# A depthwise convolution and a SiLU expert on one core: the order of a block's products, of the first blocks and of SyncE's transfers

## The chip, the cores and the metric

The kernel runs on one core of one Trainium2 chip, in float32. The metric is the device time of one execution in microseconds; lower is better. The core's engines each run their own instruction stream: TensorE (PE, with its weight loads PEld), VectorE (DVE), ScalarE (ACT), GpSimd (POOL) and SyncE (SP), which issues most DMAs here.

## The reference

A causal convolution of seven taps along the sequence, with softmaxed taps for each of eight heads, and behind it a two-layer expert with a SiLU.

```python
x: (8, 4096, 192)   weight: (8, 7)   w_in: (192, 2048)   w_out: (2048, 192)
w   = softmax(weight, axis=-1)
y[b, s, h, :] = sum_k w[h, k] * x_pad[b, s + k, h, :]     # 6 zeros ahead
h   = y.reshape(32768, 192) @ w_in
out = (h / (1 + exp(-h))) @ w_out                          # (32768, 192)
```

## The kernel before

The 32768 rows are cut into 32 blocks of 1024 (two halves of 512, which lie on the two halves of the partitions). For each block the kernel turns x into a channel-major tile `xt` (L425), adds the taps on it (L456 to L461), copies the result into `dup` (L478), forms differences of it in `win` (L495 to L511), multiplies by combined input weights, sums the results up, puts them through SiLU into `g`, and multiplies those by combined output weights. Both matrix products are done with fewer products than the plain method, in the manner of Strassen: 15 products P0 to P14 instead of 18 for each of five groups of weights, and six output products D0 to D5, for each of four quarters j and two halves e of the hidden values.

Block 0 is done plainly (`up_plain`, `down_plain`) while weights are still being rounded and combined (`rounded` on VectorE, `combine` and `combine_out` on GpSimd). From block 1 on, the order on every engine is written out by hand: `PLAN` is a list of tokens, `step(b, token)` emits one token's instructions, and `pin` keeps the instructions of an engine in the order of emission. Instructions without `pin` may be moved by the framework. A token's prefix shifts its block: none is the block b of the loop, `-` is b - 1, `=` is b - 2 and `+` is b + 1. The bars in the list have no effect on the order.

| token | what it emits | engine, line |
|---|---|---|
| `Pr.g` | product r of group g, 64 rows deep, on one half of the array | PE L583 |
| `L.nk` | the plain part of the input product | PE L595 |
| `Di.je` | output product i of quarter j, half e: four matmuls on four parts of the columns; D5 has a quarter of the width | PE L687 |
| `u`, `S`, `SL` | copy of a chain's partial sum out of its bank; SiLU | ACT L619, L631, L636 |
| `X`, `a`, `b` | sums of partial results | DVE L615 |
| `t.ji` | differences of g for the output products | DVE L123 |
| `M`, `z`, `y`, `x`, `o`, `st` | merge of the output sums, transpose back, store | DVE L758, ACT L738 to L746, DVE L768, SP L776 |
| `ld.k`, `i.k`, `ha`, `v.ki`, `sp.k`, `w.i` | for the block after: load, transpose, halo (copy and two DMAs), tap i of part k, spread into dup, window steps | SP L140, DVE L425, SP L447 and L435, DVE L458/L461 or ACT L456, SP L478, DVE L495 to L511 |

(`ld` loads the block after as well.) The products of a group run in three chains, each in one PSUM bank: 5, 2, 6, 1, 0, 14; then 3, 9, 7, 4, 8; then 12, 10. In the first chain, ScalarE copies the sum out after nearly every member (`u5` after P5, `u2` after P6 and so on), and the next product may only write when that copy is done. P13 and P11 add into a bank that an X sum has filled. P pairs run side by side when one lies on each half of the array; `ON_B` says which products lie on the second half.

Of the kernel before, what the change touches and what calls it, by code (L numbers as in the profile page):

```python
# [9 lines left out]
F32 = mybir.dt.float32  # L10
# [7 lines left out]
def kernel(  # L18
# [63 lines left out]
        "P5.0 | -P8.3 ld.1 -t.20 | -D2.10 -t.21 | -D4.11 ld.2 | -D3.10 -w.0 -a0.3 | -D5.11 | "  # L82
        "-D4.10 -S0.3 | -D0.31 -t.23 | -D3.11 -t.22 | -D2.20 i.1 | -D5.10 | -D5.20 | -D0.30 "
        "-t.30 | -D1.11 i.2 | -D4.20 -w.1 | -D4.21 -w.2 -t.31 | -D3.21 | -D2.21 i.0 | -D5.21 "
        "ha.0 -t.33 | -D3.20 | -D2.31 -t.32 | -D1.00 -w.3 | -D2.30 -w.4 | -D0.00 v.10 | "
        "-D0.10 v.00 v.01 | -D3.31 -z1.0 v.02 -y0.0 | -D5.30 | -D1.20 u5.0 -M1.0 v.11 | "
        "-D4.31 -M2.0 | -D5.31 | -D3.30 -x2.3 -x2.2 -y1.0 | P2.0 | L.02 -M3.0 -y2.0 -w.5 | "
        "-D4.30 u4.0 -M6.0 -x0.0 | P6.0 | P3.0 -M4.0 v.12 | L.00 | P5.4 u2.0 X2.0 | L.01 | "
        "P1.0 u5.4 v.03 | P9.0 | P2.4 SL.0 -M5.0 -x2.0 -x2.1 | L.10 v.04 u0.0 | L.11 -o.1 "
        "-x1.0 | L.12 u4.4 | P0.0 | P13.0 X4.0 SL.2 -M7.0 | P12.0 | P6.4 u1.0 v.20 | P3.4 | "  # L90
        "P14.0 b1.0 u2.4 S2.0 v.21 | P1.4 | P7.0 S3.0 X2.4 | P11.0 | P10.0 a5.0 | P5.1 | "
        "P9.4 S4.0 b5.0 u0.4 | P4.0 | P13.4 X4.4 u5.1 v.13 | P12.4 | P0.4 a1.0 | P2.1 | P7.4 "
        "u1.4 -o.2 | P11.4 | P8.0 b1.4 u4.1 -st.2 a5.4 S5.0 | P14.4 | P6.1 S2.4 a0.0 | P10.4 "
# [38 lines left out]
    def load(b, ks=range(NK)):  # L132
        if b not in nats:
            nats[b] = nats[b % 2] if b > 1 else xpool.tile([P, NK, TB // SQ, SQ], F32, tag="nat", name="nat", bufs=2)
        nat = nats[b]
        for k in ks:
            for i in range(P // SQ):
                c = R * k + SQ * (i % 2)
                queue = nc.scalar if not b and k == 0 and i % 2 == 0 else nc.sync
                ins = queue.dma_start(  # L140
                    out=nat[SQ * i : SQ * i + SQ, k, :, :],
                    in_=x_v[2 * b + i // 2][:, :, c : c + SQ],
                )
                if not b:
                    pin(ins)
# [286 lines left out]
    def tail_of(b):  # L432
        if (b + 1) * TT % S:
            tails[b + 1] = xpool.tile([R, NK, pad], F32, tag="tail", name="tail", bufs=2)
            nc.sync.dma_start(out=tails[b + 1], in_=xts[b][R:P, :, TB : TB + pad])  # L435

    def halo_in(b, _):
# [9 lines left out]
        nc.sync.dma_start(out=xt[R:P, :, 0:pad], in_=xt[0:R, :, TB : TB + pad])  # L447
        tail_of(b)

    def conv(b, k, i):  # L450
# [4 lines left out]
        if i == 0 and b < 2:  # L455
            pin(nc.scalar.activation(dst, src, AF.Copy, scale=tap))  # L456
        elif i == 0:
            pin(nc.vector.tensor_scalar(dst, src, scalar1=tap, scalar2=None, op0=ALU.mult))  # L458
# [9 lines left out]
    def spread(b, k):  # L468
# [77 lines left out]
    bk, us, sums, cmbs, accs = {}, {}, {}, {}, {}  # L546
# [61 lines left out]

    def sums_h(b, name, g):
# [29 lines left out]
    def sum_g(b, j, i):  # L639
# [14 lines left out]
        engine = pool if f"t.{j}{i}" in ON_POOL else vec  # L654
        engine.tensor_tensor(t[i // 2][:, i % 2, :], u, v, op=ALU.subtract)
# [117 lines left out]
    def store_out(b, i):  # L773
        for q in range((HD if b else P) // SQ):
            n, c = (i % 2, HD * (i // 2) + SQ * q) if b else (q // 2, R * i + SQ * (q % 2))
            nc.sync.dma_start(  # L776
# [270 lines left out]
```

## Time and profile before

| what | us |
|---|---|
| median of 3 runs (2412.71 to 2414.83) | 2413.17 |
| the profiled execution, its own time | 2414.33 |
| its span | 2412.6 |
| TensorE busy | 2389.5 |
| VectorE busy | 2140.6 |
| ScalarE busy | 1148.0 |
| median from issue to landing, copies into dup | 2.3 |
| the same, stores of the output | 2.0 |

The lines of the profile stand for one execution. A group's count in L583, L595 and L687 is twice the number of matmuls, since each float32 product is recorded as two passes. "Idle before" is the time that an engine had nothing to do ahead of an instruction, with what released it. Line L123 is the helper behind pinned instructions, so those are told apart by tile.

### The profile page before, as it was taken

Reading aid. Unit: us, or ns where it says so; the run is one execution under the profiler, and the core shown is the slowest. Engines: PE = TensorE matmul, PEld = TensorE weight load, DVE = VectorE, ACT = ScalarE, POOL = GpSimd, SP = SyncE. Lnnn points to the kernel's source line nnn. Section 1 sums busy time; section 2 is a strip of 40 time slices with the busy share of each in tenths; the row PEclk is TensorE's granted clock in tenths of the full one; section 3 lists DMA queues with packets and bytes.
Section 4 is the critical chain, followed back from the end, with each engine's and each line's share of the span. In section 5 each row is a group of like instructions: output and inputs, shape, how many; then the busy total and the mean of one; then the engine's idle time right before and its main releaser. Section 6 shows DMA issues by size and latency. Waiting matters only on the chain.

```text
span 2412.6 us, 43590 instructions
## 1 busy us (share of the span) xinstructions
PE 2389.5 (99%) x17630; PEld 981.1 (41%) x17630; DVE 2140.6 (89%) x2967; ACT 1148.0 (48%) x2184; POOL 116.7 (5%) x168
## 2 busy tenths in 40 slices
PE   9799999999999999999999999999999999999998
PEld 5244433444433444334444334443344443344433
DVE  8789888999888998889998889988899988899876
ACT  5145444455444554444554445544445544455443
POOL 5900000000000000000000000000000000000000
PEclk9999999999999999999999999999999999999999
DMA  7411222221222212222212222122222122221111
GB/s 150 80 38 31 37 46 41 52 46 26 45 42 48 52 31 36 46 42 51 48 24 44 42 48 51 29 39 46 42 51 49 24 44 42 48 51 29 26 33 18
DMA packets 451242, 106.54 MB, mean 44 GB/s; under 512 B 423584, under 2 KB 428704, under 8 KB 451040
## 3 DMA queue, kind: packets, MB, share of 16 engines
q1 hardware_dynamic: 447392, 101.78, 23.1%
q8 instruction: 138, 2.26, 0.4%
q0 software_dynamic: 448, 1.58, 0.3%
q10 hardware_dynamic: 3200, 0.39, 0.1%
q14 instruction: 64, 0.52, 0.1%
HBM read 31.46 MB, written 25.17 MB: 23 GB/s over the span
## 4 chain that ended last, share of the span: by engine, by line
PE 94%; DVE 4%; SPq 1%; DMA 1%; issue 0%; ACT 0%; DVEq 0%; ACTq 0%
PE ps L687 47%; PE ps L583 45%; PE ps L595 2%; DVE two L123 1%; DVE nat L461 1%; DVE mh L123 1%; DMA dup<-nat 0%; SPq L776 0%; SPq L140 0%; DMA xt<-xt 0%; DVE win L495 0%; DMA nat<-in_x_dram 0%; DVE xt L425 0%; DVE wo L123 0%; DVE t L123 0%
## 5 line engine op out<-in xcount | busy, mean ns | idle before, releaser
L583 PE MATMUL ps<-win,ws 64*128 64x512 f32 x1550 | 703.2, 610 | 13.6 <-DVE ps L615 12.9
L687 PE MATMUL ps<-g,wo 128*32 128x512 f32 x2976 | 708.7, 594 | 0.0
L583 PE MATMUL ps<-win,wr 64*128 64x512 f32 x1550 | 656.5, 609 | 0.7 <-ACT u L619 0.7
L619 ACT COPY u<-ps 128x512 f32<-128x512 f32 x775 | 450.4, 586 | 207.6 <-PE ps L583 191.4
L687 PE MATMUL ps<-t,wo 128*32 128x512 f32 (+2 forms) x4528 | 543.6, 446 | 0.0
L687 PE MATMUL ps<-t,wx 128*32 128x512 f32 x2976 | 491.7, 594 | 0.1
L631 ACT ACTIVATE g<-g 128x512 f32<-128x512 f32 x465 | 279.2, 628 | 438.8 <-DVE g L615 438.8
L461 DVE SCALAR_TENSOR_TENSOR nat<-xt,taps,nat 128x512 f32<-128x512 f32 x564 | 422.4, 754 | 7.8 <-ACT nat L456 3.8
L583 PE MATMUL ps<-dup,wr 64*128 64x512 f32 x868 | 411.4, 593 | 0.8 <-POOL wr L319 0.8
L123 DVE TENSOR_TENSOR t<-g 128x1024 f32<-128x1024 f32 x248 | 301.7, 1217 | 54.5 <-PE ps L687 53.7
L583 PE MATMUL ps<-dup,ws 64*128 64x512 f32 x682 | 345.7, 603 | 0.0
L123 DVE TENSOR_TENSOR t<-g,t 128x1024 f32<-128x1024 f32 x248 | 302.3, 1220 | 46.0 <-PE ps L687 44.9
L583 PEld LDWEIGHTS ps<-win,wr 64*128 64x128 f32 x1550 | 234.5, 186 | 234.5 <-issue 86.7
L615 DVE TENSOR_TENSOR g<-u,ps 128x512 f32<-128x512 f32 x465 | 313.7, 680 | 15.0 <-PE ps L583 14.1
L583 PEld LDWEIGHTS ps<-win,ws 64*128 64x128 f32 x1550 | 240.5, 186 | 173.4 <-DVE ps L615 64.1
L631 ACT ACTIVATE g<-ps 128x512 f32<-128x512 f32 x465 | 263.6, 596 | 56.4 <-PE ps L583 56.4
L687 PEld LDWEIGHTS ps<-t,wo 128*32 128x32 f32 x4528 | 179.2, 110 | 239.3 <-issue 228.6
L615 DVE TENSOR_TENSOR ps<-u,ps 128x512 f32<-128x512 f32 x310 | 214.0, 690 | 58.0 <-ACT u L619 26.2
L687 PE MATMUL ps<-g,wx 128*32 128x512 f32 x1488 | 246.8, 595 | 0.0
L687 PEld LDWEIGHTS ps<-t,wx 128*32 128x32 f32 x2976 | 115.5, 110 | 269.4 <-issue 261.1
L687 PEld LDWEIGHTS ps<-g,wo 128*32 128x32 f32 x2976 | 162.0, 110 | 135.4 <-issue 135.4
L746 ACT COPY cmb<-ps 96x512 f32<-96x512 f32 x30 | 17.4, 581 | 418.9 <-PE ps L687 418.9
(90 smaller groups left out, 1831.4 us busy)
## 6 DMA issues: line engine op xcount, KB each, us to landing
dup<-nat SPq DMA_DIRECT2D x345, 128.0 KB, 2.3
nat<-in_x_dram SPq DMA_DIRECT2D x382, 64.0 KB, 2.5
out_dram<-osb SPq DMA_DIRECT2D x376, 64.0 KB, 2.0
raw<-in_moe_w_out_dram SPq DMA_DIRECT2D x8, 384.0 KB, 4.0
raw<-in_moe_w_in_dram SPq DMA_DIRECT2D x12, 192.0 KB, 4.6
ws<-wr POOLq DMA_DIRECT2D x8, 192.0 KB, 4.0
raw<-in_moe_w_in_dram SPq DMA_DIRECT2D x6, 128.0 KB, 3.1
xt<-xt SPq DMA_DIRECT2D x31, 4.5 KB, 1.9
```

The costliest lines, as they stand in the source:

```text
L123: return lambda *args, **kw: pin(getattr(self.engine, name)(*args, **kw))
L461: nc.vector.scalar_tensor_tensor(out=dst, in0=src, scalar=tap, in1=dst, op0=ALU.mult, op1=ALU.add)
L583: nc.tensor.matmul(to, raw(g, *LEFT[e][r], e), rhs, start=first, stop=True, skip_group_check=True)
L595: nc.tensor.matmul(banks[PLAIN_BANKS[n and 1 + e]][:, cols], rows(wr[j] if own == e else ws[j], e)[:, a, k, :], rows(dups[b], e)[:, SLOT[e ...
L615: pin(nc.vector.tensor_tensor(out_, u, v, op=op))
L619: pin(nc.scalar.copy(us[b, g, o], t1))
L631: pin(nc.scalar.activation(h, src, AF.Silu))
L687: nc.tensor.matmul(accs[b][at][SQ * q : SQ * q + SQ, to], lhs[:, e, SQ * k : SQ * k + SQ], rhs[:, e, ts(q, TB // 4) if i == 5 else to], st ...
L746: pin(nc.scalar.copy(c[0], acc[0][0:n, :]))
```

## The change

The loop's list `PLAN` is replaced by another order of the same 300 tokens. A second list, `START`, is walked once with b = 2 and gives the order from the end of block 0 through block 2; the loop then begins at b = 3. The list `FIRST` and the mixing of block 0's output product with block 1's taps go. The first tap of every part is computed on ScalarE for all blocks, where it was on VectorE from block 2 on. All DMAs of SyncE (loads, tails, halos, spreads, stores) and the t differences are pinned, and the head of the halo is copied by pinned ScalarE instructions in blocks 1 and 2. The ten u buffers are allocated once and taken in turn from a list. Counted in D tokens, the runs of D in a block were 29, 1, 2, 2 and 14 and become 12 and 36; in `START` they are 2, 5, 11, 18, 11 and 1.

```diff
@@ -79,38 +79,72 @@
     PLAN = (
-        "P5.0 | -P8.3 ld.1 -t.20 | -D2.10 -t.21 | -D4.11 ld.2 | -D3.10 -w.0 -a0.3 | -D5.11 | "
-        "-D4.10 -S0.3 | -D0.31 -t.23 | -D3.11 -t.22 | -D2.20 i.1 | -D5.10 | -D5.20 | -D0.30 "
-        "-t.30 | -D1.11 i.2 | -D4.20 -w.1 | -D4.21 -w.2 -t.31 | -D3.21 | -D2.21 i.0 | -D5.21 "
-        "ha.0 -t.33 | -D3.20 | -D2.31 -t.32 | -D1.00 -w.3 | -D2.30 -w.4 | -D0.00 v.10 | "
...
-        "X2.2 SL.1 S1.4 v.14 | P1.2 | P9.2 S4.1 a1.1 | P5.3 | P13.2 b5.1 u0.2 X4.2 | P8.1 | "
-        "P0.2 u5.3 v.22 S0.0 | P2.3 | P12.2 u1.2 v.23 | D0.01 a0.1 u4.3 S2.2 v.06 | D0.11 "
-        "S1.0 b1.2 S5.4 | P3.3 | P6.3 t.00 S0.1 | P11.2 | P7.2 u2.3 X2.3 | P10.2 | P1.3 S4.2 "
-        "a5.2 | P9.3 | P14.2 u0.3 b5.2 | P13.3 | P4.2 X4.3 S3.2 S1.1 v.24 | P0.3 | P12.3 "
-        "S5.1 v.15 | P11.3 | P7.3 u1.3 a1.2 | D1.01 b1.3 S1.2 a5.3 S4.3 | D0.21 S2.3 t.02 | "
-        "P8.2 | P14.3 v.25 | P4.3 | P10.3 sp.0 t.01 | D1.31 a0.2 | D1.21 t.03 S0.2 | D1.10 "
-        "S3.3 S5.2 t.10 | D2.01 | D2.00 v.16 | D4.01 a1.3 sp.1 b5.3 | D3.00 v.26 S5.3 | "
-        "D0.20 S1.3 t.11 sp.2 | D4.00 | D3.01 t.12 | D1.30 +ld.0 t.13 | D5.00 | D2.11 | "
-        "D5.01"
+        "P5.0 v.20 -t.01 | -P10.3 -S3.2 | -P4.3 -S1.1 -S0.1 -sp.2 -a0.2 | -D1.31 u5.0 -t.03 "
+        "-S4.3 | -D2.01 -S2.3 -t.02 | -D2.00 | -D0.00 -b5.3 | -D4.00 -a1.3 -S5.3 -t.10 -S5.4 "
+        "| -D3.01 -S0.2 -S5.2 | -D5.00 -w.0 | -D1.00 v.00 -t.11 -S1.2 | -D0.31 | -D1.30 -w.1 "
+        "| -D4.01 | -D2.10 -t.13 | -P8.3 | P2.0 v.11 | -D5.01 u4.0 v.01 | -D3.00 -S1.3 -t.12 "
+        "| -D4.10 | -D4.11 -t.20 | -D2.11 | -D3.10 -t.22 | -D5.11 | -D0.10 -a0.3 | -D0.11 "
...
+        "-D5.31 -M3.0 | -D5.21 | -D5.30 | -D4.30 -w.5 -M6.0 | -D5.20 | -D4.31 -x2.2 -x0.0 "
+        "-M4.0 | P3.0 | P6.0 -x2.0 -x2.1 v.15 | L.01 | P5.4 u2.0 -M5.0 | L.00 | P1.0 X2.0 "
+        "u5.4 v.26 | L.02 | P2.4 u0.0 v.04 | P0.0 | P9.0 SL.0 -w.4 -x1.0 | L.10 u1.0 X4.0 | "
+        "L.12 u4.4 -o.1 | L.11 -x2.3 | P14.0 | P13.0 v.16 -st.1 SL.2 -o.3 | P11.0 | P7.0 "
+        "S3.0 | P6.4 | P12.0 +ld.2 S4.0 a5.0 S2.0 | P5.1 | P3.4 b1.0 u2.4 | P4.0 | P10.0 "
...
+        "b5.1 u0.2 | P11.1 | P9.2 u2.3 a0.1 | P0.2 | P12.2 +i.1 S4.1 +ha.0 X4.2 | P1.3 | "
+        "P3.3 u1.2 b1.2 | P11.2 | P7.2 u0.3 -st.3 X2.3 S1.4 | P10.2 | P0.3 a5.2 S4.2 | P9.3 "
+        "-st.0 | P14.2 b5.2 u1.3 S5.1 -o.2 | P13.3 | P4.2 X4.3 -st.2 | P12.3 | P14.3 a1.2 | "
+        "P7.3 | P11.3 b1.3 S3.3 sp.0 +v.10 | P8.2 a5.3"
     )
-    ON_POOL = "".split()
+    START = (
+        "=i.2 =i.0 =i.1 =ha.0 -ld.2 =v.00 =v.10 =v.01 -ld.1 =v.20 =v.11 =v.21 =v.12 -ld.0 "
+        "=v.22 =v.23 =v.13 =v.14 =v.15 =v.02 =v.16 =v.24 =sp.1 =v.03 =v.25 =v.26 =v.04 =sp.2 "
+        "=v.05 =v.06 -i.2 =sp.0 -i.0 ld.1 =w.0 =w.1 =o.0 -i.1 -L.01 -P5.0 =w.2 -ha.0 -L.02 "
+        "-P5.4 -u5.0 =w.3 -P3.0 -P2.0 -u5.4 =w.5 =o.1 -L.00 -P2.4 -u4.0 =w.4 =st.1 -P6.0 "
+        "-u4.4 -SL.0 -P6.4 -u2.0 -X2.0 -L.11 -u2.4 -L.10 -v.10 -P12.0 -P1.0 -v.11 -L.12 -u0.0 "
+        "=o.2 -P9.0 -P1.4 -v.20 =st.2 -SL.2 -P13.0 -P0.0 -u0.4 -X4.0 -v.12 -P0.4 -P3.4 -u1.0 "
+        "ld.0 -S2.0 -b1.0 -P7.0 -P14.0 -u1.4 -X2.4 -P11.0 -P10.0 -S3.0 -a5.0 =st.0 -P5.1 "
+        "-P9.4 -S4.0 -b5.0 -v.13 -P12.4 -P4.0 -u5.1 ld.2 -X4.4 -v.00 -P2.1 -P14.4 -b1.4 -a1.0 "
...
+        "-S5.0 -P7.2 -P11.2 -v.24 -S0.1 -P9.3 -P14.2 -b1.2 -S5.4 -a5.2 -S1.4 -P10.2 -P1.3 "
+        "-S3.2 -v.25 -S5.1 -D0.00 -v.15 -S4.2 -v.05 -u0.3 -D1.00 -b5.2 -P0.3 -P13.3 -X4.3 "
+        "-v.16 -P12.3 -P4.2 -u1.3 -t.00 -P11.3 -P7.3 -a1.2 -D1.20 -b1.3 -S1.2 -D0.11 -a5.3 "
+        "-S2.3 -S4.3 -t.02 -D0.01 -S5.2 -D1.01 -v.26 -t.01 -D0.31 -v.06 -P10.3 -P14.3 -t.03 "
+        "-P8.2 -P4.3 -S3.3 -sp.2 -D1.21 -a0.2 -a1.3 -D1.30 -b5.3 -sp.1 -D0.21 -t.10 -S5.3 "
+        "-S0.2 -D4.00 i.1 -D3.01 i.0 +ld.2 i.2 -D4.01 -t.11 -D2.00 ha.0 -D2.01 -D0.20 -sp.0 "
+        "-t.12 -D3.00 -t.13 v.00 -D5.00 v.20 P5.0 -P8.3 -D5.01 -a0.3 -D2.10 -t.20 -S0.3 +ld.0 "
+        "-D5.11 -D4.10 -S1.3 v.21 v.10 -D1.10 u5.0 -w.0 -D2.11 -t.21 -D0.10 -w.1 -D3.10 v.01 "
...
+        "P1.3 S2.2 b1.2 P7.2 P11.2 -st.1 u0.3 X2.3 S1.4 P10.2 P14.2 +i.2 S4.2 a5.2 P0.3 P9.3 "
+        "+i.1 P13.3 P4.2 u1.3 X4.3 +ha.0 S5.1 b5.2 P14.3 P7.3 a1.2 P11.3 P12.3 S3.3 sp.0 a5.3 "
+        "S0.4 P8.2 b1.3 +v.10 -st.3"
+    )
     QUEUE = (0, 4, 1, 2, 3)
-    FIRST = (
-        ". | . | . | v.10 | . | v.11 | . | v.12 | . | v.13 | . | v.14 | . | v.15 | . | v.16 | "
-        ". | v.20 sp.1 | . | v.21 | . | v.22 | . | v.23 | . | v.24 | . | v.25 | . | v.26 | . "
-        "| sp.2 | . | . | . | . | . | . | . | . | w.0 | w.1 | w.2 | w.3 | w.4 | w.5 | . | ."
-    )
...
                 c = R * k + SQ * (i % 2)
                 queue = nc.scalar if not b and k == 0 and i % 2 == 0 else nc.sync
-                ins = queue.dma_start(
-                    out=nat[SQ * i : SQ * i + SQ, k, :, :],
-                    in_=x_v[2 * b + i // 2][:, :, c : c + SQ],
-                )
-                if not b:
-                    pin(ins)
+                pin(
+                    queue.dma_start(
+                        out=nat[SQ * i : SQ * i + SQ, k, :, :],
+                        in_=x_v[2 * b + i // 2][:, :, c : c + SQ],
+                    )
+                )
...
-            nc.sync.dma_start(out=tails[b + 1], in_=xts[b][R:P, :, TB : TB + pad])
+            pin(nc.sync.dma_start(out=tails[b + 1], in_=xts[b][R:P, :, TB : TB + pad]))
...
-            if b == 2:
+            if b <= 2:
                 pin(nc.scalar.copy(head, tails.pop(b)))
             else:
                 nc.gpsimd.tensor_copy(head, tails.pop(b))
-        nc.sync.dma_start(out=xt[R:P, :, 0:pad], in_=xt[0:R, :, TB : TB + pad])
+        pin(nc.sync.dma_start(out=xt[R:P, :, 0:pad], in_=xt[0:R, :, TB : TB + pad]))
         tail_of(b)
...
-        if i == 0 and b < 2:
+        if i == 0:
             pin(nc.scalar.activation(dst, src, AF.Copy, scale=tap))
-        elif i == 0:
-            pin(nc.vector.tensor_scalar(dst, src, scalar1=tap, scalar2=None, op0=ALU.mult))
...
-                    nc.sync.dma_start(out=rows(dups[b], e)[:, slot, :], in_=rows(src, n))
+                    pin(nc.sync.dma_start(out=rows(dups[b], e)[:, slot, :], in_=rows(src, n)))
...
+    us, free = {}, []
+
+    def used(*key):
+        free.append(us.pop(key))
+        return free[-1]
+
...
-            us[b, g, o] = upool.tile([P, TB], F32, tag="u", name="u")
+            us[b, g, o] = free.pop(0)
             pin(nc.scalar.copy(us[b, g, o], t1))
         elif name[0] == "X":
-            add(banks[XBANK[o]], us.pop((b, g, o)), t2)
+            add(banks[XBANK[o]], used(b, g, o), t2)
         elif name[0] == "a":
...
-        engine = pool if f"t.{j}{i}" in ON_POOL else vec
-        engine.tensor_tensor(t[i // 2][:, i % 2, :], u, v, op=ALU.subtract)
+        pin(nc.vector.tensor_tensor(t[i // 2][:, i % 2, :], u, v, op=ALU.subtract))
...
-            nc.sync.dma_start(
-                out=out_v[2 * b + n][:, :, c : c + SQ], in_=osbs[b][SQ * q : SQ * q + SQ, i, :, :]
+            pin(
+                nc.sync.dma_start(
...
-        if (b, token) == (1, "ha.0"):
-            assert not any(t[0] == "D" for c, t in did if c == 1)
-            for j in range(NJ):
-                combine_out(j)
...
-        y, x_ = (upool.tile([P, TB], F32, tag="u", name="u") for _ in range(2))
+        y, x_ = free[0:2]
...
-    ahead = [f"i.{k}" for k in range(NK)] + ["ha.0"] + [f"v.0{i}" for i in range(K)]
-    for t in ahead:
-        step(0, t)
     for g in (0, 1, 4, 2, 3):
         for e in range(2):
             combine(g, e)
-    step(0, "sp.0")
-    load(2)
-    beside = FIRST.split("|")
-    for _, s in zip_longest(down_plain(0), beside, fillvalue=""):
-        for t in s.split():
-            step(0, t)
-    for k in range(NK):
-        turn_out(0, k)
-        store_out(0, k)
-    did.update((0, t) for t in base if t[0] not in "ivw")
-    did.update((1, t) for t in base if t[:2] == "ld")
-
-    banks = [bank() for _ in range(8)]
+    ahead = {"i", "ha", "v", "sp", "w"}
+    outs = {f"{t}.{k}" for t in ("o", "st") for k in range(NK)}
+    did.update((0, t) for t in base if t.split(".")[0] not in ahead and t not in outs)
+
+    def first_down():
+        for _ in down_plain(0):
+            pass
+        for j in range(NJ):
+            combine_out(j)
+        banks.extend(bank() for _ in range(8))
+        free.extend(upool.tile([P, TB], F32, tag="u", name="u") for _ in range(10))
+
     begun = set()
-    for b in range(1, NB + 2):
+    for t in START.split():
+        if not banks and (t[:2] in ("-P", "-L", "=o")):
+            first_down()
+        step(2, t)
+    for b in range(3, NB + 2):
         for s in plan:
             for t in s:
                 step(b, t)
```

## The prediction

> **What bounds the kernel now.** I read the page first (busy shares and the forty slices), then the chain of waits, whole and for one block, then the timeline of each engine around the one hole that the slices show, and last the table by stage for the clock in that hole.
>
> ```profile
> PE 2389.5 (99%) x17630; PEld 981.1 (41%) x17630; DVE 2140.6 (89%) x2967; ACT 1148.0 (48%) x2184; POOL 116.7 (5%) x168
> PE   9799999999999999999999999999999999999998
> ```
>
> TensorE is busy 99% of the span; one slice, the second, is at 7. VectorE is close behind at 89%, ScalarE has half of its time free. So a gain must come from TensorE: from the hole, or from time in which it is "busy" but not at its rate. The chain of waits for the block at 930 to 1012 us shows the latter (start, length, line; L583 is the products P, L687 the output products D, a "x" counts half products, since each product is recorded as two passes):
>
> ```profile
> 959.34 1.85 PE ps L687 x16
> 961.20 6.33 PE ps L583 x28
> 967.52 1.85 PE ps L687 x16
> 969.38 1.92 PE ps L583 x8
> 971.29 10.88 PE ps L687 x112
> 982.17 1.06 PE ps L583 x4
> 983.23 21.19 PE ps L687 x232
> ...
> 1005.48 0.99 PE ps L687 x8
> ```
>
> Inside one kind, passes start every 0.429 us (timeline: 971.68, 972.11, then 972.96, 973.39), two P side by side, four parts of a D side by side. So a pair of P, or one D, takes 0.858 us, and a D5 a quarter of it. By that, x16 of D (two tokens) should take 1.72 and takes 1.85; x8 of P (two pairs) should take 1.72 and takes 1.92; x4 should take 0.86 and takes 1.06. A D run thus costs 0.13 to 0.14 extra and a P run 0.20: **0.34 us for each change to D and back**. The old list has five D runs in a block (of 29, 1, 2, 2 and 14 tokens), hence 1.7 us. The whole of it: 75 P at 0.429, six L at 0.429, 40 D at 0.858 and 8 D5 at 0.215 make 70.8 us; the period is 73.71 (first long P run of the second block at 127.03, of the last at 2338.23, thirty periods). Of the 2.9 us over, 1.7 are changes of kind and 1.2 are short waits of P for ScalarE's and VectorE's copies and sums.
>
> The hole:
>
> ```profile
> 108.44 1.02 PE L583 MATMUL ps<-win,ws 64*128 64x512 f32 x2
> 122.39 1.22 PE L583 MATMUL ps<-win,ws 64*128 64x512 f32 x1 [12.93 <-DVE ps L615]
> ...
> 106.69 6.34 SPq L776 DMA_DIRECT2D out_dram<-osb  x12
> 113.14 0.63 SPq L447 DMA_DIRECT2D xt<-xt  x1
> ...
> 115.14 1.25 DVE L458 TENSOR_SCALAR nat<-xt,taps 128x512 f32<-128x512 f32 x2 [5.51 <-DMA xt<-xt]
> 116.42 5.32 DVE L461 SCALAR_TENSOR_TENSOR nat<-xt,taps,nat 128x512 f32<-128x512 f32 x4
> 121.65 0.68 DVE L615 TENSOR_TENSOR ps<-u,ps 128x512 f32<-128x512 f32 x1
> ```
>
> Read it backwards. TensorE waits 12.93 us for an X sum (L615); that sum stands on VectorE behind six taps of block 2; those wait 5.51 us for the halo copy (L447); and the halo copy stands on SyncE behind twelve stores of block 0. The hole costs more than itself:
>
> ```profile
> 113.80:122.30 8.50, 0.00 (x0) 0.00 (x0) 7.06 (x8) 0.00 (x0) 7.88 (x14) 0.50 0.20 29
> 122.40:127.30 4.90, 4.90 (x18) 3.22 (x20) 3.13 (x4) 0.78 (x2) 2.99 (x4) 0.50 0.02 3
> 127.50:131.50 4.00, 4.00 (x20) 1.74 (x18) 2.41 (x4) 2.16 (x4) 0.00 (x0) 1.00 0.01 2
> ```
>
> The granted clock (third number from the end) is at 0.50 in the hole and for the first 5.0 us after it (122.4 to 127.4), then 1.00.
>
> **The change, part by part.**
>
> **1. The new loop list.** It has the same 300 tokens, only reordered: D now comes in runs of 12 and 36. Two changes and back instead of five: 3 x 0.34 = **1.02 us less a block**. Neighbouring P on the same half of the array, which cannot run side by side, fall from 14 to 6; most of them are made up by the next pair, so I take 0.1 us less (0 to 0.4).
>
> What it can cost: a P of the long chain (5, 2, 6, 1, 0, 14 of a group) must wait until ScalarE has copied the sum that the one before it left in the bank. One link needs 0.86 (the product) + about 0.2 (the recorded 0.589 of a pass beyond its 0.429, and the semaphore) + 0.586 (the copy, L619) + 0.1 (the weights, not loaded ahead; a pass after such a wait is recorded at 0.693 instead of 0.589), so 1.8 us. Counted in the lists at 0.429 a P, 9 of 25 links were shorter than that (8 at 1.72, one at 1.29) and 8 will be (6 at 1.72, two at 1.29). The second link at 1.29 is short by 0.5, two at 1.72 are saved at 0.1 each: 0.3 more. Also, the two short D runs were pauses of 1.7 us in which ScalarE and VectorE caught up; they are gone: 0.1. Together **0.4 us more** (bounds 0 and 1.0, the latter if every link lost another 0.03 to 0.04). Net 1.02 + 0.1 - 0.4 = **0.72 us a block**, over the 29 periods that follow block 2: **20.9 us**.
>
> **2. First taps on ScalarE.** Three taps a block leave VectorE (0.48 us recorded, 0.44 start to start, so 1.3 us a block) and cost ScalarE 0.72 recorded, 0.63 start to start (timeline at 81.2), so 1.9 us. ScalarE is at 35 us of 73.7. Two of the three stand among the D, where ScalarE waits for sums anyway (page: its second kind of L631 waits 438.8 us in all), the third at the end of the P stage. I take 0; without that cover each delays a copy by up to 0.63, 1.9 us a block. For VectorE the 1.3 us is off the path: it had 7.9 us idle in a block. The wait that is added: ScalarE now stands at a tap until the halo copy lands, and u copies queue behind it, and P behind those.
>
> **3. The start.** The list for blocks 1 and 2 puts the halo copy of block 2 ahead of block 0's twelve stores, X2.0 ahead of the taps on VectorE, and the first taps on ScalarE. From the rows: the subtractions start at 101.0 when the spreads have landed; two of them at 0.86, a transpose out and one in at 0.66 end at about 104; the halo copy takes 0.63 to issue and 1.9 to land, 106.6; ScalarE reaches the first tap after u2.4, about 107.5. So nothing should stand there. The stores come later, into a queue that has nothing urgent: 12 x 0.53 us of SyncE's time, hidden. That takes away **12.93 us**, and the slow clock after it. On that the Trainium skill ("TensorE: Matmul & The Clock Gate", "What's actually happening") says that the full clock returns after about 3.4 us of sustained work; by that rule 1.7 us would be lost at half rate. The row shows 5.0 us at 0.50, so **2.5 us** lost, and the row decides. With no idle stretch of some us left, both go: **15.4 us**.
>
> What is given back: VectorE is then full in block 1's P stage. It has 35 sums at 0.60, six window steps at 0.65, six transposes at 0.65 and the 13 taps listed ahead of D0.00 at 0.67 (up to 0.97 beside GpSimd, whose weight sums still run to 117): 37.5 to 41.4 us against 36 for TensorE. GpSimd's sums for group 4 made P wait at 104.69 (0.65) and at 107.48 (0.80); P5.4 is now the fourth product, so this may grow by up to 3 us. The list has six D runs in this block, one more than before: 0.34. I take **3 us** (bounds 0 and 8). Net **12.4 us**.
>
> **4. SyncE pinned; fixed u buffers.** The DMAs keep the list's order. The tightest place is sp.2, whose two copies for slots 1 and 3 must land before w.0: seven D later, 5.4 us, against 4 x 0.6 to issue + 2.3 to land = 4.7. It holds by 0.7. Free u buffers are the same ten: 0. The end (finish) is as before: 0 (within 1 us: the D of the first two groups no longer stand among the last P).
>
> **Sum**: 20.9 + 12.4 = 33.3 us. The profiled execution took 2414.33 (span 2412.6 and 1.7 around it), which goes to about 2381.0; it lies 1.2 above the median of the three runs, 2413.17, which goes to **2380**.
>
> **The rivals.**
> (a) *The undivided P stage waits no more than before and nothing is given back at the start*: 1.12 x 29 + 15.4 = 47.9, so 2365. For it: two list orders that both keep most links over 1.8. Against: VectorE at 37 to 41 us of 36.
> (b) *The pauses were worth what the changes cost*: nine more waits of 0.1 a block. Then only the start gains: 2401. For it: the row of 1.2 us of short waits sits wholly in the P stage. Against: the link counts, 9 and 8.
> (c) *The hole only moves* (ScalarE stands at a tap for the halo, or GpSimd's weights are late): only the loop gains, 2392.
> (d) *Slower*: w.0 is the place. If sp.2's copies, now pinned among SyncE's DMAs, land late, VectorE stands at w.0, and t.11 behind it; D2.10, five tokens after w.0, needs t.11. There are four D in between, 3.4 us, and VectorE takes 0.65 + 1.15 for w.0 and t.11, so 1.6 us of room. From 0.7 + 1.6 = 2.3 us of lateness on, every further us goes onto TensorE in every block. The gains of 33.3 us are 1.15 a block, so at 3.5 us late (5.8 from issue to landing) the kernel is as before, and at 3.8 us late some 9 us slower, 2422. Against: median landing 2.3 us, the DMA engines at 1 to 2 tenths, and VectorE has seven other tokens of its own before w.0.
> That the reordering does nothing is excluded for the loop: TensorE follows the list.
>
> **How the numbers follow.** Forecast 0.62 (its own range 2370 to 2391), (a) 0.15, (b) 0.13, (c) 0.05, (d) 0.05. The range 2363 to 2398 holds the forecast, (c), nearly all of (a) and a little of (b). This kernel's runs can tell about 0.2%, 5 us, from no change. All but (d) and the edge of (b) are faster by more: 0.94, within 0.02, slower 0.04.
>
> **What would show it.** In the chain of a block: L687 in two runs of x96 and x288 (some records can be missing), the first after six P passes; the period between equal places of two blocks at 73.0. At 100 to 130 us: clock 1.00 throughout, no TensorE idle over 2 us, the halo copy issued before block 0's first store. ScalarE's busy time up by about 60 us, VectorE's down by about 40. The prediction is wrong if the period stays above 73.5 (then look at what P waits for: ScalarE's u is (b), VectorE's win is (d)), or if a slice near 110 us is again under 9.

## The result, and the profile after

| | before | changed |
|---|---|---|
| median, us | 2414.0 (2412.71 to 2415.26) | 2378.24 (2378.21 to 2378.31) |
| the profiled execution, its span | 2412.6 | 2376.6 |
| period of a block in the loop | 73.71 | 72.80 |
| VectorE busy in all | 2140.6 | 2107.6 |
| ScalarE busy in all | 1148.0 | 1199.2 |

The ratio is 0.9852 (0.9835 to 0.9869), so the change takes 35.8 us away. On another chip the changed kernel ran again: 2377.85 against 2413.91.

The page of the changed kernel, busy times and TensorE's forty slices. The second slice, which stood at 7, is now at 9:

```profile
PE 2366.9 (100%) x17630; PEld 1058.5 (45%) x17630; DVE 2107.6 (89%) x2877; ACT 1199.2 (50%) x2275; POOL 99.1 (4%) x167
PE   9999999999999999999999999999999999999998
```

The chain of waits around one block of the loop (start, length, line; the output products D are now L724, the products P L615, the plain part L627):

```profile
231.46 26.56 PE ps L724 x288
258.02 1.06 PE ps L615 x4
...
264.04 29.36 PE ps L615 x131
293.40 9.80 PE ps L724 x96
303.20 1.06 PE ps L615 x4
304.25 26.56 PE ps L724 x288
```

D stands in two runs, x96 and x288, which are 12 and 36 tokens, and the same place of the next block comes 72.79 us later (304.25 - 231.46). The period was 73.71.

The start of the changed kernel, rows of several engines' timelines ("idle before", with its releaser, in brackets):

```profile
104.65 0.64 SPq L481 DMA_DIRECT2D xt<-xt  x1
...
107.67 5.47 SPq L814 DMA_DIRECT2D out_dram<-osb  x8
...
109.04 0.72 ACT L490 ACTIVATE nat<-xt,taps 128x512 f32<-128x512 f32 x1
...
115.81 2.25 DVE L493 SCALAR_TENSOR_TENSOR nat<-xt,taps,nat 128x512 f32<-128x512 f32 x1
...
119.78 3.17 DVE L493 SCALAR_TENSOR_TENSOR nat<-xt,taps,nat 128x512 f32<-128x512 f32 x3
...
118.72 0.69 PE L615 MATMUL ps<-win,ws 64*128 64x512 f32 x1 [0.78 <-DVE ps L653]
...
123.60 1.29 PE L615 MATMUL ps<-win,wr 64*128 64x512 f32 x3 [1.09 <-DVE g L653]
```

The halo copy is issued at 104.65, ahead of the first store (107.67); the first tap on ScalarE at 109.04 shows no idle time before it. Of the hole of 12.93 us two gaps are left, 0.78 and 1.09 us, both released by VectorE. The table by stage (columns: stretch, its length, then busy time and count of PE, PEld, DVE, ACT, POOL, then the granted clock, the DMA share and GB/s) shows that the clock no longer falls:

```profile
100.00:118.60 18.60, 17.93 (x78) 7.74 (x74) 15.91 (x22) 12.97 (x25) 17.05 (x31) 1.00 0.59 97
118.60:124.80 6.20, 4.99 (x21) 2.19 (x23) 6.18 (x10) 3.98 (x8) 4.64 (x6) 1.00 0.27 42
```

**Where the 36.0 us between the two spans came from.** From the chain before and after: 29 periods that are shorter by 0.884 on average (the mean period after is 72.82, since one or two blocks of a run take 73.14) give 25.6 us; the tail is 0.1 us longer; the start therefore gives 10.5 us. The prediction had 20.9, 0 and 12.4.

### The profile page after: what moved, and what is told of

It reads as the page before. It is cut to its first block, busy times and chain, and to the rows that moved or that the text cites. A ratio compares the mean times of both kernels' runs of the same rounds, so it can differ in the third digit from the quotient of the medians.

```text
span 2376.6 us, 44012 instructions
## 1 busy us (share of the span) xinstructions
PE 2366.9 (100%) x17630; PEld 1058.5 (45%) x17630; DVE 2107.6 (89%) x2877; ACT 1199.2 (50%) x2275; POOL 99.1 (4%) x167
## 4 chain that ended last, share of the span: by engine, by line
PE 99%; DVE 0%; ACT 0%; issue 0%; ACTq 0%
PE ps L724 47%; PE ps L615 43%; PE ps L627 4%; PE ps L743 2%; PE ps L565 2%; PE ps L977 1%; PE ps L417 0%; DVE nat L493 0%; DVE g L653 0%; DVE cmb L157 0%; ACT u L157 0%; DVE t L692 0%; DVE osb L157 0%; DVE ps L653 0%; DVE u L653 0%
## 5 line engine op out<-in xcount | busy, mean ns | idle before, releaser
L615 PE MATMUL ps<-win,ws 64*128 64x512 f32 x1550 | 699.3, 609 | 0.8 <-DVE ps L653 0.8
L724 PE MATMUL ps<-g,wo 128*32 128x512 f32 x2976 | 681.2, 592 | 0.0
L615 PE MATMUL ps<-win,wr 64*128 64x512 f32 x1550 | 636.8, 598 | 1.1 <-DVE g L653 1.1
L657 ACT COPY u<-ps 128x512 f32<-128x512 f32 x775 | 444.7, 586 | 284.3 <-PE ps L615 281.7
L724 PE MATMUL ps<-t,wo 128*32 128x512 f32 (+2 forms) x4528 | 524.2, 447 | 0.0
L724 PE MATMUL ps<-t,wx 128*32 128x512 f32 x2976 | 489.9, 592 | 0.6 <-DVE g L653 0.6
L493 DVE SCALAR_TENSOR_TENSOR nat<-xt,taps,nat 128x512 f32<-128x512 f32 x564 | 414.5, 754 | 5.8 <-ACT nat L490 4.3
L615 PE MATMUL ps<-dup,wr 64*128 64x512 f32 x868 | 412.6, 597 | 0.0
L615 PE MATMUL ps<-dup,ws 64*128 64x512 f32 x682 | 338.5, 603 | 0.0
L653 DVE TENSOR_TENSOR g<-u,ps 128x512 f32<-128x512 f32 x465 | 314.8, 682 | 15.2 <-PE ps L615 7.4
L615 PEld LDWEIGHTS ps<-win,wr 64*128 64x128 f32 x1550 | 239.0, 186 | 173.2 <-issue 96.3
L780 ACT COPY yx<-ps 32x512 f32<-32x512 f32 x150 | 86.9, 579 | 423.9 <-PE ps L724 422.4
L615 PEld LDWEIGHTS ps<-win,ws 64*128 64x128 f32 x1550 | 245.4, 186 | 121.9 <-ACT u L657 62.2
L724 PEld LDWEIGHTS ps<-t,wo 128*32 128x32 f32 x4528 | 178.3, 110 | 244.3 <-issue 233.2
L653 DVE TENSOR_TENSOR ps<-u,ps 128x512 f32<-128x512 f32 x310 | 212.5, 686 | 40.5 <-PE ps L615 28.3
L724 PE MATMUL ps<-g,wx 128*32 128x512 f32 x1488 | 246.2, 594 | 0.0
L724 PEld LDWEIGHTS ps<-t,wx 128*32 128x32 f32 x2976 | 121.0, 110 | 261.2 <-issue 231.4
L724 PEld LDWEIGHTS ps<-g,wo 128*32 128x32 f32 x2976 | 169.3, 110 | 112.1 <-issue 112.1
```

The lines of the kernel that those rows point to most:

```text
L493: nc.vector.scalar_tensor_tensor(out=dst, in0=src, scalar=tap, in1=dst, op0=ALU.mult, op1=ALU.add)
L615: nc.tensor.matmul(to, raw(g, *LEFT[e][r], e), rhs, start=first, stop=True, skip_group_check=True)
L653: pin(nc.vector.tensor_tensor(out_, u, v, op=op))
L724: nc.tensor.matmul(accs[b][at][SQ * q : SQ * q + SQ, to], lhs[:, e, SQ * k : SQ * k + SQ], rhs[:, e, ts(q, TB // 4) if i == 5 else to], st ...
L780: pin(nc.scalar.copy(to, acc[3 * (name[0] == "x") + k][n:P, :]))
```

## The experiments

All differences are to the kernel before on the same chip; the changed kernel stands at -35.8 and, on the other chip, at -36.1.

| kernel | median, us | ratio (interval) | to before | loop period |
|---|---|---|---|---|
| changed, second time | 2377.85 | 0.9852 (0.9839 to 0.9866) | -36.1 | 72.80 |
| e1_three_runs | 2396.56 | 0.9925 (0.991 to 0.994) | -18.1 | 73.44 |
| e11_late_run | 2396.62 | 0.993 (0.9917 to 0.9944) | -17.3 | 73.44 |
| e2_taps_dve | 2391.47 | 0.9904 (0.9889 to 0.9919) | -23.2 | 73.21 |
| e10_one_tap_act | 2384.60 | 0.9881 (0.9867 to 0.9894) | -29.3 | 73.01 |
| e8_old_taps_act (from the kernel before) | 2418.17 | 1.0015 (1.0008 to 1.0022) | +4.0 | 73.76 |
| e3_stores_first | 2380.99 | 0.986 (0.9844 to 0.9877) | -33.7 | |
| e4_before_halo_first (from the kernel before) | 2409.40 | 0.9982 (0.9975 to 0.9989) | -4.7 | |
| e5_unpinned | 2382.10 | 0.9864 (0.9849 to 0.9879) | -32.0 | 72.79 |
| e6_taps_later | 2379.56 | 0.9855 (0.984 to 0.987) | -35.1 | |
| e7_taps_spread | 2377.35 | 0.9848 (0.9833 to 0.9863) | -36.8 | |
| e9_searched | 2401.49 | 0.995 (0.9936 to 0.9964) | -12.4 | 73.64 |

### What a change between P and D costs

**e1_three_runs** splits the run of 36 D: two products go into its middle, all else stays.

```diff
-  "-D0.20 -t.30 | -D0.01 | -D4.20 -y0.0 -t.31 -z1.0 | "
+  "-D0.20 -t.30 | P3.0 | P6.0 | -D0.01 | -D4.20 -y0.0 -t.31 -z1.0 | "
...
-  "-D4.31 -x2.2 -x0.0 -M4.0 | P3.0 | P6.0 -x2.0 -x2.1 v.15 | L.01 | P5.4 u2.0 -M5.0 | "
+  "-D4.31 -x2.2 -x0.0 -M4.0 | -x2.0 -x2.1 v.15 | L.01 | P5.4 u2.0 -M5.0 | "
```

> The changed kernel, with the two products P3.0 and P6.0 moved from behind the 36 output products into the middle of them (after D0.20), in the loop's list only: three runs of D in a block instead of two, and nothing else. Theory (each change to D and back costs TensorE 0.31 us, measured in the kernel before as 0.117 + 0.104 + 0.085): 29 blocks at 0.31, 9 us more than the changed kernel, about 2387. Rival (the pause lets ScalarE and VectorE catch up, so the short waits fall by as much): within 3 us of the changed kernel, 2376 to 2381.

Its chain of waits in the same place of a block:

```profile
1039.77 12.02 PE ps L723 x124
1051.80 1.06 PE ps L614 x4
1052.85 13.88 PE ps L723 x152
```

The pair of P should take 0.86 us and takes 1.06. Counting the starts of the passes against their regular distance of 0.429 us, P3.0 starts 0.113 and 0.104 us late in its two passes, and the first D behind it 0.097: **0.31 us for the change to P and back**. But the period grew by 0.64. The rest is at another place: P1.0, which follows P6.0 in its chain, starts 0.35 us late, where it was 0.04 in the changed kernel. The two parts, 0.31 each, make up the growth. Neither theory had the sum: the price of the change was right, the whole was not.

**e11_late_run** asks whether that second half belongs to a change as such. Only two D are cut off, so that the same two products stand almost where they stood:

```diff
-  "-D5.30 | -D4.30 -w.5 -M6.0 | -D5.20 | -D4.31 -x2.2 -x0.0 -M4.0 | P3.0 | P6.0 -x2.0 "
+  "-D5.30 | -D4.30 -w.5 -M6.0 | P3.0 | P6.0 | -D5.20 | -D4.31 -x2.2 -x0.0 -M4.0 | -x2.0 "
```

> The changed kernel with the last two output products of the run of 36 (D5.20 and D4.31) moved behind P3.0 and P6.0, so that D runs are 12, 34 and 2, in the loop's list only; P3.0, P6.0 and what follows keep their order and the product chain gets a pause, not less room. Theory (a change to D and back costs 0.29 us, as between D0.20 and D0.01 in the first experiment, where the other 0.35 was a wait of P1.0): 8 us more, 2385 to 2388. Rival (each change costs 0.6, as that whole experiment): 2395 to 2398. Second rival (the pause pays for itself): 2377 to 2381.

The change itself costs 0.113 + 0.105 + 0.096 = 0.31 us, and P1.0 is again 0.35 us late; the period is again 73.44. ScalarE's and TensorE's timelines name what P1.0 waits for:

```profile
1066.14 0.26 ACT L774 COPY yx<-ps 32x128 f32<-32x128 f32 x1 [4.07 <-PE ps L723]
1066.41 0.58 ACT L779 COPY yx<-ps 32x512 f32<-32x512 f32 x1
1067.00 0.52 ACT L774 COPY yx<-ps 32x128 f32<-32x128 f32 x2
1067.55 1.10 ACT L656 COPY u<-ps 128x512 f32<-128x512 f32 x2
...
1065.13 0.59 PE L614 MATMUL ps<-win,ws 64*128 64x512 f32 x1
...
1068.19 0.69 PE L614 MATMUL ps<-win,ws 64*128 64x512 f32 x1
```

P6.0's second pass starts at 1065.13 and is over at 1065.72. The copy of its sum (u2.0) could follow, but it stands in ScalarE's list behind four copies of output sums (yx), the first of which waits 4.07 us for the D that were moved behind P6.0. So u2.0 starts at 1067.55 and P1.0, which may only write after it, at 1068.19. In the changed kernel P3.0 and P6.0 follow the last D, and the yx copies run beside them. A split thus costs 0.3 us for itself and as much again where it takes this cover away.

### The first taps

**e2_taps_dve** puts the first taps of block 2 and later back on VectorE, with the new lists.

```diff
-        if i == 0:
+        if i == 0 and b < 2:
...
+        elif i == 0:
+            pin(nc.vector.tensor_scalar(dst, src, scalar1=tap, scalar2=None, op0=ALU.mult))
```

> The changed kernel with the first taps from block 2 on back on VectorE (tensor_scalar), all else as it is. Theory (VectorE has about 8 us idle in a block, so 1.3 us more a block is hidden): 2378 to 2382. Rival (VectorE is full in the undivided product stage, so its 1.3 us a block land on TensorE): up to 38 us more, 2400 to 2416.

It lost 12.6 us of the 35.8. One period of the changed kernel by its table by stage:

```profile
1020.10:1092.89 72.80, 72.80 (x554) 32.86 (x552) 65.33 (x90) 37.52 (x72) 0.11 (x1) 1.00 0.23 43
```

And one of this kernel, in the same view:

```profile
1025.57:1098.78 73.21, 73.20 (x555) 32.77 (x553) 66.41 (x94) 35.73 (x70) 0.11 (x1) 1.00 0.23 43
```

VectorE has 1.1 us more to do (66.41 against 65.33) and even so 6.8 us idle in the period, and the period is 0.41 us longer. By the starts of the passes, two places around the end of the stage of products lose it. Both stand behind a tap that VectorE now does ahead of a sum (timelines of VectorE and TensorE):

```profile
1025.15 0.48 DVE L492 TENSOR_SCALAR nat<-xt,taps 128x512 f32<-128x512 f32 x1
1025.55 0.68 DVE L655 TENSOR_TENSOR g<-u,ps 128x512 f32<-128x512 f32 x1
1026.14 0.48 DVE L492 TENSOR_SCALAR nat<-xt,taps 128x512 f32<-128x512 f32 x1
...
1027.67 0.68 DVE L655 TENSOR_TENSOR g<-u,ps 128x512 f32<-128x512 f32 x1
...
1026.28 0.69 PE L617 MATMUL ps<-win,ws 64*128 64x512 f32 x1
...
1028.41 0.63 PE L726 MATMUL ps<-t,wx 128*32 128x512 f32 x3
```

The tap v.10 (1025.15) delays a sum, and P4.3 starts when that sum is over (1026.28); its two passes are together 0.20 us later than in the changed kernel. The tap v.20 (1026.14) delays the sum at 1027.67, and D2.01, the second D of the run of 12, starts when that is over (1028.41), 0.22 us late, where it was on time. The two make up the 0.41; v.00, which stands further on among the D, costs nothing. The theory that the taps are worth nothing falls.

**e10_one_tap_act** leaves only v.10, a tap at the end of the P stage, on ScalarE and puts v.00 and v.20 back. (The expectation has both of these among the D. v.00 is; v.20 stands at P5.0, just ahead of the D.)

```diff
-        if i == 0:
+        if i == 0 and (b < 2 or k == 1):
...
+        elif i == 0:
+            pin(nc.vector.tensor_scalar(dst, src, scalar1=tap, scalar2=None, op0=ALU.mult))
```

> The changed kernel with two of the three first taps from block 2 on back on VectorE (v.00 and v.20, which stand among the output products) and only v.10 left on ScalarE (it stands at the end of the product stage, ahead of the last sums that P10.3 and P8.3 wait for). With all three on VectorE the block was 0.41 us longer. Theory (the place decides, not VectorE's load): the block stays at 72.8 to 72.9, 2378 to 2381. Rival (VectorE's load decides, two of three taps are two thirds of it): 73.07, 2386 to 2388.

The period is 73.01: half of the 0.41 is back. By the starts of the passes, P4.3 is again as in the changed kernel (0.05 us late in its two passes, 0.26 in e2), and D2.01 is late by 0.2 us as in e2. So the place decides: v.10 and v.20 cost about 0.2 us each, each at the one product that waits for the sum behind it, and v.00 nothing. The theory knew only the first of the two places; that the number lies nearer to the rival's 73.07 is chance.

**e8_old_taps_act** does this part alone, on the kernel before.

```diff
-        if i == 0 and b < 2:
+        if i == 0:
...
-        elif i == 0:
-            pin(nc.vector.tensor_scalar(dst, src, scalar1=tap, scalar2=None, op0=ALU.mult))
```

> The kernel before with only the first taps from block 2 on moved to ScalarE; the old lists stay. Theory, from the run of the changed kernel with these taps on VectorE (0.45 us a block): about half of that or less, as the old list gives VectorE pauses, so 0 to 0.3 us a block, and the hole a little shorter by 1.1 us: 2403 to 2414. Rival (ScalarE's taps stand ahead of u copies in a list that was not made for them): slower than before, 2415 to 2425.

It is 4.0 us slower. The loop does not gain (73.76 against 73.71), and at the start ScalarE is what stands at a tap:

```profile
115.91 1.33 ACT L456 ACTIVATE nat<-xt,taps 128x512 f32<-128x512 f32 x2 [13.76 <-DMA xt<-xt]
117.15 0.56 ACT L617 COPY u<-ps 128x512 f32<-128x512 f32 x1
```

The u copy queues behind the tap, P behind the copy: TensorE's hole grows from 12.93 to 15.30 us. So the taps on ScalarE need the new order, while the order brings most of its gain without them. The new order without the taps gives 0.50 us a period (73.71 to 73.21), the taps without the new order nothing, and the taps on top of it 0.41.

### The start

**e4_before_halo_first** takes the twelve stores from in front of the halo copy in the kernel before, and nothing else: they are issued right behind the halo copy of block 2, and both are pinned.

```diff
-        nc.sync.dma_start(out=xt[R:P, :, 0:pad], in_=xt[0:R, :, TB : TB + pad])
+        pin(nc.sync.dma_start(out=xt[R:P, :, 0:pad], in_=xt[0:R, :, TB : TB + pad]))
...
         if (b, token) == (1, "ha.0"):
+            for k in range(NK):
+                store_out(0, k)
...
     for k in range(NK):
         turn_out(0, k)
-        store_out(0, k)
```

> The kernel before, with block 0's twelve stores issued behind block 2's halo copy instead of ahead of it; VectorE's order is untouched, so the X sums still stand behind six taps. Theory (the hole is two waits in a row: 5.5 us for the halo copy and 6.5 us of taps ahead of the X sum): the hole of 12.93 us shrinks to 6 to 8 us, the slow clock after it stays, 5 to 7 us less than the kernel before, 2407 to 2409. Rival (the stores are the whole cause): hole and slow clock go, 15 us less, 2399.

The timelines of SyncE, VectorE and TensorE in its hole:

```profile
110.67 0.62 SPq L447 DMA_DIRECT2D xt<-xt  x1
112.07 6.61 SPq L776 DMA_DIRECT2D out_dram<-osb  x12
...
112.67 1.11 DVE L458 TENSOR_SCALAR nat<-xt,taps 128x512 f32<-128x512 f32 x2 [2.06 <-DMA xt<-xt]
113.83 5.18 DVE L461 SCALAR_TENSOR_TENSOR nat<-xt,taps,nat 128x512 f32<-128x512 f32 x4
118.93 0.68 DVE L615 TENSOR_TENSOR ps<-u,ps 128x512 f32<-128x512 f32 x1
119.67 1.22 PE L583 MATMUL ps<-win,ws 64*128 64x512 f32 x1 [11.24 <-DVE ps L615]
```

The halo copy starts only 2.5 us earlier (110.67 instead of 113.14), for what it copies comes late from VectorE, behind the window steps and block 0's output. The X sum still stands behind six taps, and TensorE still waits 11.24 us. The edit is worth 4.7 us by the medians; the profiled execution is the slowest of the 18 (2411.56), so its hole is rather too long for them. What is left of the hole is put down to VectorE's order by this row; no run moved the X sums alone.

**e3_stores_first** does the reverse in the changed kernel: all of block 0's stores ahead of the halo.

```diff
-  "=sp.0 -i.0 ld.1 =w.0 =w.1 =o.0 -i.1 -L.01 -P5.0 =w.2 -ha.0 -L.02 "
+  "=sp.0 -i.0 ld.1 =w.0 =w.1 =o.0 -i.1 -L.01 -P5.0 =w.2 =o.1 =o.2 =st.0 =st.1 =st.2 -ha.0 -L.02 "
```

> The changed kernel with block 0's last two transposes and its twelve stores put ahead of block 2's halo copy in the start list, as the old kernel had them on SyncE; the X sums stay ahead of the taps. Theory (the halo copy behind the stores is half of the hole): the halo lands 7 to 9 us later, at 114 to 116 us, ScalarE stands at the first tap from 109 on with the u copies queued behind it, TensorE stops for 4 to 6 us[...]: 5 to 9 us more, 2383 to 2387. Rival (the hole came only from the X sums that stood behind the taps on VectorE): 2378 to 2380.

It costs 2.1 to 2.4 us, less than the theory's 5 to 9. ScalarE stands at the first tap for 4.43 us, as expected; TensorE waits 2.85 us at 114.9 for the u copy behind it, and is then at half rate, by the table by stage (clock third from the end):

```profile
114.40:121.20 6.80, 6.30 (x14) 3.62 (x16) 5.99 (x6) 4.08 (x8) 6.57 (x11) 0.50 0.44 70
```

With VectorE's order right, late stores are thus a small matter.

**e5_unpinned** takes the pins off SyncE's DMAs.

```diff
-                pin(
-                    queue.dma_start(
+                    queue.dma_start(
...
-        pin(nc.sync.dma_start(out=xt[R:P, :, 0:pad], in_=xt[0:R, :, TB : TB + pad]))
+        nc.sync.dma_start(out=xt[R:P, :, 0:pad], in_=xt[0:R, :, TB : TB + pad])
```

> The changed kernel with the pins of loads, tails, halos, spreads and stores on SyncE taken off again, so that the framework may order these DMAs; all else as it is. Theory (in the loop SyncE has slack, 0; at the start the framework may again put stores ahead of the halo copy, as it did before, about 3 us): 2378 to 2382. Rival (the loop's spreads come late behind loads or stores, and the window steps with them): over 2390.

In the loop the pins are worth nothing (72.79). At the start it is slower by some 4 us, and at another place than thought: the framework put GpSimd's weight sums in another order, and TensorE waits for one (timeline of TensorE, then the table by stage for the 3.4 us behind it, at half clock).

```profile
107.22 0.69 PE L615 MATMUL ps<-dup,wr 64*128 64x512 f32 x1 [3.89 <-POOL wr L353]
```

```profile
108.20:111.60 3.40, 3.40 (x9) 1.27 (x6) 0.00 (x0) 1.17 (x2) 3.01 (x8) 0.51 0.48 73
```

One of its four times was 2377.99, that of the changed kernel, the others 2381.7 to 2382.88; why they differ is open.

**e6_taps_later** goes after the two gaps that were left: the four taps that stood beside GpSimd's last sums move behind them.

```diff
-  "-P9.4 -S4.0 -b5.0 -v.13 -P12.4 -P4.0 "
+  "-P9.4 -S4.0 -b5.0 -P12.4 -P4.0 "
...
-  "-P7.4 -P11.4 -u4.1 -v.14 -S3.4 -P6.1 -P10.4 -S1.0 -v.21 -P8.0 -P5.2 -v.01 -u2.1 "
+  "-P7.4 -P11.4 -u4.1 -S3.4 -P6.1 -P10.4 -S1.0 -P8.0 -P5.2 -u2.1 "
```

The tokens v.21 and v.01 go ahead of v.22, and v.13 and v.14 behind P8.4.

> The changed kernel with four taps of block 2 (v.13, v.14, v.21, v.01) moved to about 124 to 127 us in the start list, behind GpSimd's last weight sums, which end at 123.4. Theory (a tap beside GpSimd's sums takes 1.1 to 2.2 us instead of 0.74, and this made the two gaps of 0.78 and 1.09 us on TensorE at 118.7 and 123.6): both gaps close, 1.5 to 2.5 us less, 2376 to 2377. Rival (VectorE is simply full in block 1, and four taps later are as bad as four taps sooner): 2378 or more.

The taps take 0.70 us each, and both gaps are gone, but five of them now stand in a bundle, and the X sum behind them is late (timelines of VectorE and TensorE):

```profile
123.45 3.52 DVE L492 SCALAR_TENSOR_TENSOR nat<-xt,taps,nat 128x512 f32<-128x512 f32 x5
126.89 0.69 DVE L652 TENSOR_TENSOR ps<-u,ps 128x512 f32<-128x512 f32 x1
...
127.63 1.05 PE L614 MATMUL ps<-win,wr 64*128 64x512 f32 x1 [2.06 <-DVE ps L652]
```

The table by stage from there on:

```profile
127.80:131.20 3.40, 3.40 (x10) 1.89 (x12) 2.66 (x5) 0.00 (x0) 0.00 (x0) 0.51 0.00 0
131.30:135.00 3.70, 3.70 (x19) 1.88 (x18) 2.77 (x6) 3.49 (x7) 0.00 (x0) 1.00 0.00 0
```

The wait of 2.06 us brought a half clock of 3.4 us with it (0.51, then 1.00), and it is 0.7 to 1.0 us slower than the changed kernel.

**e7_taps_spread** puts the same taps there, but never more than two together; the taps behind them (v.22 to v.24 and v.02 to v.04) move on by one place each.

```diff
-  "-u1.1 -v.22 -P9.1 -P14.1 -P8.4 -X4.1 -S3.1 -b1.1 -u4.2 -P7.1 -P5.3 -v.02 -S0.0 "
+  "-u1.1 -v.13 -P9.1 -P14.1 -P8.4 -v.14 -X4.1 -S3.1 -b1.1 -u4.2 -P7.1 -P5.3 -v.21 -S0.0 "
...
```

> The changed kernel with block 2's taps v.13, v.14, v.21, v.01 of the start list taken out of the time of GpSimd's last sums (116 to 123.4 us) and the taps of the following 15 us moved on one place each, so that never more than two stand together. Theory (a tap beside GpSimd's sums costs up to 2.2 us, and in the last attempt five taps in a bundle made the new gap): both gaps of TensorE at 118.7 and 123.6 go and no new one over 0.5 us comes, 2375.5 to 2377.5. Rival (VectorE lacks the time wherever the taps stand): 2378 or more.

The first two of them in VectorE's timeline, 1.53 us for both:

```profile
123.34 1.53 DVE L492 SCALAR_TENSOR_TENSOR nat<-xt,taps,nat 128x512 f32<-128x512 f32 x2
```

The gaps at 118.7 and 123.6 are gone; a new one of 0.69 us stands at 136.53. It is the fastest version, by 0.7 us against the changed kernel's repeat and 1.0 against its first run, each taken against the kernel before on its chip. The times of single executions overlap (2376.88 to 2378.11, and 2377.52 to 2378.31), so it is not told apart from it.

**e9_searched** has that start, and a loop list reordered so that my count of waits came out lowest (all 300 tokens, only their order):

```diff
-  "P5.0 v.20 -t.01 | -P10.3 -S3.2 | -P4.3 -S1.1 -S0.1 -sp.2 -a0.2 | -D1.31 u5.0 -t.03 "
+  "P5.0 | v.20 | -t.01 | -P10.3 | -a0.2 | -S5.4 | -sp.2 | -S4.3 | -P4.3 | -D0.00 | -D0.31 "
...
```

> The start list of the last run with four taps spread, and a loop list reordered further by small moves of single tokens that keep every dependence and the runs of 12 and 36 D: moves picked by a count of where a product waits for a copy or a sum. By that count 0.1 us of a block's short waits go; theory: 72.7 us a block instead of 72.8, 2373.5 to 2376.5. Rival (the short waits only move to other products): 2377 to 2379.

It failed: 73.64 where 72.7 was expected. One thing that the count had missed is that VectorE's window steps then stand waiting for the transfers into dup, in 27 of the blocks (waits view: us in total, times, longest):

```profile
DVE win L529 <- DMA dup<-nat: 39.0, 27, 2.9
```

But this is not the loss: from block to block these waits are between 0.3 and 2.3 us long, and the period is 73.64 or 73.65 with all of them. Only with the two longest, 2.6 and 2.9 us, is it more, 73.90 and 74.17 (one other block took 73.94, with a wait of 0.4). What is late in the blocks that I counted stands behind VectorE again (timelines of VectorE and TensorE):

```profile
1061.00 2.07 DVE L495 SCALAR_TENSOR_TENSOR nat<-xt,taps,nat 128x512 f32<-128x512 f32 x3
1062.99 1.22 DVE L694 TENSOR_TENSOR t<-g 128x1024 f32<-128x1024 f32 x1
...
1064.26 1.92 PE L726 MATMUL ps<-t,wo 128*32 128x512 f32 x16
```

The difference t.32 stands behind three taps, and D3.31 (1064.26), which needs it, is 0.33 us late. P5.4 and L.01, the first products behind P6.0 and P3.0, are late by 0.27 and 0.37 us, behind VectorE's sums of the output. That is most of the 0.84 us a period.

**The changed kernel again**, beside the last of these on their chip:

> The changed kernel itself once more, on the same chip as the three beside it, so that differences of 1 to 3 us can be told: 2378 to 2379.

It took 2377.85, 0.4 us less than in its first run.

## Why the prediction was right, and where it was not

The time, 2378 where 2380 was predicted, came out of terms that were partly wrong and made up for each other: the loop gave 4.7 us more than its 20.9, the start 1.9 less than its 12.4. That it lies so near is in part luck.

**1. The loop list: mechanism right, two terms mis-sized.** The runs x96 and x288 are there. A change and back costs 0.31 us (e1, e11, and by the starts of the passes in the kernel before as well), not the 0.34 read from the lengths in the chain; three fewer are 0.94 us, where 1.02 stood. The order alone gave 0.50 (e2 against before), and the step said 0.72. In e2 the price of the changes less the gain is 0.94 - 0.50 = 0.44, close to the 0.4 that the step took for additional waits, but by luck: 0.41 of it is P4.3 and D2.01 behind VectorE's late sums, not the chain of links and the lost pauses from which the term was built. With the taps on ScalarE it is gone. Counted with 0.31 a change, the waits other than changes of kind are 73.70 - 70.79 - 1.57 = 1.3 us a block before and 72.80 - 70.79 - 0.63 = 1.4 after: the additional waits were about 0. (The 0.1 us for neighbours on the same half cannot be read from this.)

**2. The taps: "I take 0" is the step that failed.** They are worth 0.41 us a period, 11.9 us over 29 periods, a third of all that the change brings. The bound that was given went the wrong way: it priced ScalarE, which has room, and took VectorE's 1.3 us as off the path since 7.9 us in a block were idle. The idle time is real (6.8 us in e2) but stands in other places than the end of the P stage, where P4.3 and D2.01 wait for VectorE's last sums. The step also had v.20 among the D, where it stands ahead of them. The wait of ScalarE for the halo, which the step named, did not come with the new order (109.04, no idle), and came in full with the old one (e8).

**3. The start: 10.5 us for 12.4.** The hole and the slow clock went, as predicted: 15.4 us. What is given back is 4.9 and not 3 (10.5 = 15.4 - 4.9). Part of it are the gaps of 0.78 and 1.09 us, where taps beside GpSimd took 2.25 us and three took 3.17; the step had allowed "up to 0.97". It also had GpSimd's weight sums end at 117. Those of the input weights do, but those of the output weights behind them run to 124.9 in the kernel before (to 123.4 in the changed one), beside the taps. Most of the remaining 3 us lie between 123.60 and 193.01 us: 59 P, six L and all 48 D of block 1 stand there, 63.9 us at the regular distance, and they took 69.4. That is 5.5 us over, where a whole block of the old loop has 2.9. Six changes of kind at 0.31 are 1.9 of it; the rest are short waits, which I did not take apart. Read backwards, the chain of causes had named the stores on SyncE at its far end; e4 and e3 put them at 4.7 and 2.1 to 2.4 us, and leave the rest, by difference, to VectorE's order.

**4. Pins and u buffers: 0, right for the loop** (72.79 without pins). At the start the version without them is some 4 us slower in three of its four times, with a wait for GpSimd in the profiled one; the step had no term for that.

The rivals: (a) assumed waits no worse and nothing given back, and the loop did go its way, at 0.88 a period against its 1.12. (b), pauses worth what the changes cost, is excluded by the period. (c), the hole only moves, is what e8 shows for the old order, and nothing of it is in the new one. (d), late spreads at w.0, did not come: in the changed kernel the window steps wait for a transfer into dup once, for 1.1 us. e9, in another order, fits the room of 2.3 us that (d) gave: waits up to 2.3 us cost nothing, 2.6 and 2.9 us cost 0.25 and 0.5.

## What to carry to other kernels

An engine with a tenth of its time idle can still set the time, if the work before its deadline has no slack: price moved work at the place where others wait for that engine, not against its idle time over the period. Two edits of which one makes the other's cover have to be priced together: here one alone costs 4 us and is worth 12 on top of the other. And a hole is read backwards to its end only by removing one cause at a time; the last DMA in the chain was the smaller part.

## What the runs showed of the hardware that I had not expected

**A tap on VectorE beside GpSimd's sums takes 1.06 to 2.25 us** where it takes 0.70 to 0.75 alone. It reads two tiles from SBUF; VectorE's sums with one operand in PSUM (L653) stayed at 0.67 to 0.69 at the same time. GpSimd pays too: its last three sums took 3.04 us beside taps, 1.70 when e6 and e7 had moved them away. The Trainium skill ("SBUF — State Buffer", "Who interferes with whom") says that a VectorE instruction with two SBUF inputs contends with a GpSimd instruction that reads SBUF, for a pair of ports that only one of them can hold. Both figures agree with that; that this port is the cause was not tried by itself.

**Short idleness can halve TensorE's clock.** A wait of 2.06 us (e6) was followed by 3.4 us at 0.51, one of 2.85 us (e3) by 6.8 us at 0.50, one of 3.89 us (e5) by 3.4 us at 0.51; waits of 0.78 and 1.09 us left it at 1.00. The skill ("TensorE: Matmul & The Clock Gate", "What's actually happening") speaks of an idle window of about 3.4 us; here less than two thirds of it sufficed.
